# PSUM tiles by row pair, an earlier way out, and whole-array products for the first chunk in a convolution-and-feed-forward kernel

## The chip, the cores and the metric

The kernel runs on one core of a Trainium2 chip. The metric is the device time of one execution in microseconds (us); of several timed executions the median is given.

## The reference, cut to what matters

The input `x` has 4 sequences of 4096 tokens with 192 numbers each. A softmax over 7 taps, one set for each token and each of 8 heads, weighs the token and the six before it; a two-layer network with 2048 hidden units follows.

```python
w = softmax(weight_gen, axis=-1)                  # (4, 4096, 8, 7)
out[b, s, h, :] = sum over k of w[b, s, h, k] * x_pad[b, s + k, h, :]   # 6 zero rows ahead
h = out.reshape(16384, 192) @ w_in                # 192 -> 2048
g = maximum(0.01 * h, h)
y = g @ w_out                                     # 2048 -> 192
```

## The kernel before, in words

**Tiling.** Each of the 128 partitions owns 128 consecutive tokens. A chunk is 4 of these rows for all partitions, 512 tokens; there are 32 chunks (`NCH`). The inner size is cut into 16 blocks of 128 (`NF`), taken two at a time, which gives 8 steps for a chunk (`NQ`) and 256 in all (`NP`). Step q is step i = q mod 8 of chunk c = q div 8; its two blocks are numbers 2q and 2q+1.

**Precision.** Each fp32 value goes to TensorE as the sum of two parts, `h` and `l`. The first product (`mm1`) needs h·h, h·l and l·h for three blocks of 64 of the 192 inputs. The second (`mm2_pass`) multiplies the high part of the activations (`g_h`) by both parts of `w_out` (384 columns) and the low part (`g_l`) by the high one (192 columns).

**TensorE (PE).** All products but the first transposes use the array as two halves of 64 rows, which work at the same time on different PSUM banks. The second product of one block is made in four passes. In pass i the upper half works on one of the four rows of tokens and the lower half on another; passes 0 and 1 give each row one half of its sum, passes 2 and 3 the other. I call the two matmul pairs of one block in one pass (384 columns, then 192) a *set*; a block has 4 sets, a chunk 64. Passes 0 and 1 (`mm2_first`) end a step, passes 2 and 3 (`mm2_second`) follow the first product of the next step. Between them `tell` places a nop on SyncE (SP) that waits for the last matmul of pass 1; pass 2 waits for this nop. SP also issues nearly all DMAs, in order.

**A chunk's boundary.** `firsts` says which blocks a step begins. Step i = 1 begins none, it finishes the old chunk's last two blocks and then calls `evacuate`; step i = 2 begins four blocks of the new chunk. The sums of four rows lie in one PSUM tile of four banks (`po`, one buffer). `evacuate` takes rows 0 and 2 as one strided slice and rows 1 and 3 as another: ScalarE (ACT) copies the low columns to `ot`, VectorE (DVE) adds the high ones, one DMA stores four rows.

**Activations.** `act(n)` is a Prelu in place in PSUM and a copy to `g_h` on ACT, then a subtraction to `g_l` on DVE. PSUM holds four tiles `hp` of the first product; `g_h` and `g_l` have six buffers each.

**The next chunk's input.** The convolution runs on GpSimd (POOL). Its result is split (`split_h` on ACT, `split_l` on POOL), transposed in blocks of 32 on DVE (`squares`), and spread over the partitions by 16 DMAs from SP into `xx` (`spread_squares`, four for each k). From chunk 2 on a chunk's convolution result is split at i = 1, squared at i = 2 and spread at i = 3 to 6 of the chunk before it.

**The start.** The weights arrive as 64-bit numbers and are rounded and split by ACT, DVE and POOL while chunk 0 is computed. The order of all this work is written out by hand in `START`: a letter is one piece of work, `s` is the next step. `x` and `X` spread chunks 1 and 2, `m` and `Y` are their last squares, `v` and `V` their `split_l`, `w` widens a weight block and issues a later block's load on SP, `o` and `O` round, `q` is one operation of a convolution on POOL. The tile framework makes an instruction wait for earlier ones that touch the same part of a tile, or, for a new tile, the same buffer.

Of the kernel before, what the change touches and what calls it, by code (L numbers as in the profile page):

```python
# [24 lines left out]

C0 = 1

START = "ASgdeddeedddggedregpwpdgdrwegggekeodgggeedoegrgedupedlprruwTrowlpulwsKwroupOswlpuLopsrUlOwrppsuOrwlupowrrOulwwlrOuplpoMscuwutlrwvosumrEowlorLulwuODquqqqqLqqxssqLqqqqqssssCyVqqqqsqqqqqqqYqqXsss"


@with_exitstack
def conv_attention_moe_kernel(
# [291 lines left out]
                    start=(m == 0), stop=(m == len(passes) - 1),  # L324
                )

    def act(n):

        t = hp.pop(n)
        nc.scalar.activation(out=t, in_=t, func=AF.Prelu, alpha=0.01)  # L330
        g_h[n] = gp.tile([P, TOK], F32R, tag="gh", name="gh")
        g_l[n] = gp.tile([P, TOK], F32R, tag="gl", name="gl")
        h, l = g_h[n], g_l[n]
        if n >= NF:
            t = t.rearrange("p (k j t) -> p j k t", k=NK, j=J)
            h, l = (g.rearrange("p (j k t) -> p j k t", k=NK, j=J) for g in (h, l))
        nc.scalar.copy(out=h, in_=t)  # L337
        nc.vector.tensor_tensor(out=l, in0=t, in1=h.bitcast(F32), op=ALU.subtract)  # L338

    po = {}  # L340
    count = dict(mm2=0)
    after = mybir.DependencyInfo(mybir.DependencyClass.Sync, mybir.DependencyReason.DATA)
    HALF = J // 2

    def mm2_pass(ns, i, told=None):

        rows = range(J)[::1 if count["mm2"] % 2 else -1]
        for n in ns:  # L350
            f = n % NF
            for g, d in ((g_h, 2 * D), (g_l, D)):
                for u, s in enumerate(HALVES):
                    j = rows[(i + u * HALF) % J]
                    ins = nc.tensor.matmul(  # L355
                        out=po[0][:, j, 0:d],
                        lhsT=g[n][s, j * P:(j + 1) * P], rhs=wo[s, f, 0:d],
                        start=(f == 0 and i < HALF and g is g_h),
                        stop=(f == NF - 1 and i >= HALF and g is g_l),
                        skip_group_check=True,  # L360
                    ).ins
                    if told is not None:
                        tc.add_manual_dep(ins, told.name, after, reason="rows left")
                        told = None
        return ins
# [7 lines left out]
    def mm2_first(ns):  # L373


        if ns[0] % NF == 0:
            po[0] = ps_o.tile([P, J, TOK], F32, tag="o", name="po")
        count["mm2"] += 1
        for i in range(HALF):
            ins = mm2_pass(ns, i)  # L380
        return tell(ins)

    def mm2_second(ns, told):
        for i in range(HALF, J):
            mm2_pass(ns, i, told if i == HALF else None)
        for n in ns:
            del g_h[n], g_l[n]

    def last_products(ns):

        count["mm2"] += 1
        told = [None] * HALF
        for i in range(J):
            ins = mm2_pass(ns, i, told[i - HALF] if i >= HALF else None)
            if i < HALF:
                told[i] = tell(ins)

    def evacuate(c, last=False):


        ot = op.tile([P, J, D], F32, tag="ot", name="ot")
        r = row_of(c)
        even, odd = slice(0, J, 2), slice(1, J, 2)
        for i, js in enumerate((even, odd) if count["mm2"] % 2 else (odd, even)):
            nc.scalar.copy(out=ot[:, js], in_=po[0][:, js, D:2 * D])  # L405
            nc.vector.tensor_tensor(  # L406
                out=ot[:, js], in0=po[0][:, js, 0:D], in1=ot[:, js], op=ALU.add
            )
            if last:
                eng = (nc.sync, nc.scalar)[i]  # L410
                eng.dma_start(out=out_rows[:, r + js.start:r + J:2, :], in_=ot[:, js])
        if not last:
            nc.sync.dma_start(out=out_rows[:, r:r + J, :], in_=ot)

    order = [(0, IN), (1, IN), (2, IN), (0, OUT)]
    for q in range(3, NQ):
# [18 lines left out]
    with tc.manual_schedule():  # L435
# [31 lines left out]

        def firsts(q):

            c, i = divmod(q, NQ)  # L470
            if i == 1 or q == 0:
                return []
            if i == 0:
                return list(range(2 * q - (4 if c == 1 else 2), 2 * q))
            if c == 0:
                return [2 * q - 4, 2 * q - 3]
            if q == NP - 1:
                return []
            return list(range(2 * q - (4 if i == 2 else 2), 2 * q))

        def step(q):

            c, i = divmod(q, NQ)
            if i == 0 and c in sm_q:
                load_weights(sm_q[c])
                load_rows(sm_q[c])
            if i == 1 and c in sm_q:
                softmax_max(sm_q[c])
                softmax_sub(sm_q[c], nc.gpsimd)
            begun, told = pending.pop() if pending else (None, None)  # L490
            mm1(q)


            if c != 1 or i != 1:
                act(2 * q)
# [4 lines left out]
            if c == 1 and i == 1:  # L500
                act(2 * q)
            act(2 * q + 1)
            ns = firsts(q)
            if ns:
                pending.append((ns, mm2_first(ns)))
            if c > 1:
                if i == 0:
                    feed(c + 1, 2 * K)
                if c + 1 < NCH:
                    if i == 1:  # L510
                        split_h(c + 1)
                        split_l(c + 1, nc.gpsimd)
                    if i == 2:
                        squares(c + 1, 0)
                        squares(c + 1, 1)
                    if 3 <= i < 3 + NK:
                        spread_squares(c + 1, [i - 3])
# [8 lines left out]
        w0 = ps_o.tile([P, J, TOK], F32, tag="o", name="w0")  # L526
# [7 lines left out]
        n = 0  # L534
        for what in START:
            if what in stages:
                prepare(what)
# [26 lines left out]
            elif what in "cC":  # L564
                split_h(1 + "cC".index(what))
            elif what in "vV":
                split_l(1 + "vV".index(what), nc.gpsimd)
            elif what in "tm":
                squares(1, "tm".index(what))
            elif what in "yY":  # L570
                squares(2, "yY".index(what))
            elif what in "xX":
                spread_squares(1 + "xX".index(what))
            elif what == "s":
                step(n)
                n += 1
# [37 lines left out]
```

## Time and profile before

| | |
|---|---|
| median of 3 runs | 1223.44 us (1222.64 to 1223.48) |
| profiled execution | 1225.84 us, its span 1224.1 us |
| mean granted TensorE clock | 0.988 |
| PE busy | 1159.2 us, 95% of the span |
| POOL / ACT / DVE busy | 798.5 (65%) / 655.7 (54%) / 518.5 (42%) us |
| chain that ended last | PE 83%, DVE 5%, ACT 5%, SP's queue 3%, DMA 2%, issue 2% |

Busy time is a share over the whole span; of a matmul the start is recorded and the end modelled, so that the distance from start to start tells what a matmul takes out of the stream. The chain that ended last is followed back from the last instruction to what released it, step by step.

### The profile page before, as it was taken

The page shows a single profiled execution, that of the slowest core. Times are in us where ns is not written, and L with a number is a line of the kernel's source. Part 1 is how long each engine was busy: PE and PEld are TensorE (multiplying, and loading weights), DVE is VectorE, ACT ScalarE, POOL GpSimd, SP SyncE. Part 2 cuts the span into 40 slices and gives each one's busy share as a digit, 9 for nine tenths or more (in the row PEclk, how much of TensorE's full clock was granted, in tenths as well). Part 3 has the DMA queues.
Part 4 walks back from the last instruction along what each step waited for, and adds up shares of the span by engine and source line. Part 5 has one row for each costly group of instructions (what it writes and reads, how often), then busy time and mean ns, then how long its engine had stood idle before and what let it go on. Part 6 is the DMA issues. An engine that isn't in the chain of part 4 may idle for free.

```text
span 1224.1 us, 30487 instructions
## 1 busy us (share of the span) xinstructions
PE 1159.2 (95%) x12812; PEld 1047.6 (86%) x12812; DVE 518.5 (42%) x857; ACT 655.7 (54%) x1187; POOL 798.5 (65%) x511
## 2 busy tenths in 40 slices
PE   2778999999999999999999999999999999999997
PEld 1667988999889898898898988888889989898887
DVE  7753343344444343444343444434344433443432
ACT  3645455455555555555555555545555554555553
POOL 7778666776666678666677766658766667965300
PEclk9799999999999999999999999999999999999999
DMA  6342032322313242232323313232231323222120
GB/s 195 104 118 66 28 106 65 106 66 52 106 50 108 53 118 67 53 96 52 116 53 84 92 48 106 53 105 66 67 99 49 103 66 105 66 54 52 47 59 14
DMA packets 39366, 95.29 MB, mean 78 GB/s; under 512 B 9407, under 2 KB 17087, under 8 KB 37438
## 3 DMA queue, kind: packets, MB, share of 16 engines
q1 hardware_dynamic: 38542, 92.77, 27.4%
q8 instruction: 100, 1.64, 0.6%
q10 hardware_dynamic: 688, 0.59, 0.2%
q14 instruction: 36, 0.29, 0.1%
HBM read 31.98 MB, written 12.58 MB: 36 GB/s over the span
## 4 chain that ended last, share of the span: by engine, by line
PE 83%; DVE 5%; ACT 5%; SPq 3%; issue 2%; DMA 2%; DVEq 0%; ACTq 0%
PE po L355 45%; PE hp L322 38%; DVE ot L406 3%; SPq L305 2%; ACT ot L405 2%; ACT gh L337 1%; ACT hp L330 1%; DMA xx<-sq 1%; DVE gl L338 0%; DMA wi_raw<-in_moe_w_in_dram 0%; DVE t L118 0%; DVE t L116 0%; DVE bits L122 0%; DVE acc L250 0%; DMA wt<-in_weight_gen_dram 0%
## 5 line engine op out<-in xcount | busy, mean ns | idle before, releaser
L355 PE MATMUL po<-wo,gh 64*128 64x384 f32 x4096 | 615.7, 356 | 21.9 <-SPq L369 11.1
L338 DVE TENSOR_TENSOR gl<-hp,gh 128x512 fp32r<-128x512 f32 x512 | 354.0, 691 | 666.8 <-ACT gh L337 666.4
L330 ACT ACTIVATE hp<-hp 128x512 f32<-128x512 f32 x512 | 301.3, 589 | 458.2 <-PE hp L322 458.2
L355 PE MATMUL po<-wo,gl 64*128 64x192 f32 x4096 | 535.2, 250 | 0.8 <-DVE gl L338 0.6
L322 PE MATMUL hp<-xx,wi_h 64*128 64x512 f32 x3072 | 514.5, 400 | 14.7 <-DVE bits L122 4.5
L355 PEld LDWEIGHTS po<-wo,gh 64*128 64x128 f32 x4096 | 411.6, 185 | 45.6 <-PE hp L322 23.6
L355 PEld LDWEIGHTS po<-wo,gl 64*128 64x128 f32 x4096 | 414.1, 188 | 13.0 <-DVE gl L338 1.8
L250 POOL TENSOR_TENSOR acc<-acc,tmp 128x768 f32<-128x768 f32 (+1 forms) x191 | 346.9, 1816 | 14.3
L322 PEld LDWEIGHTS hp<-xx,wi_h 64*128 64x128 f32 x3072 | 300.9, 186 | 60.9 <-DVE gl L338 6.0
L322 PE MATMUL hp<-xx,wi_l 64*128 64x512 f32 x1536 | 334.0, 394 | 0.0
L337 ACT CAST gh<-hp 128x512 fp32r<-128x512 f32 x512 | 300.7, 587 | 48.0 <-PE po L355 33.0
L240 POOL TENSOR_TENSOR tmp<-xt,wt 128x768 f32<-128x768 f32 (+1 forms) x192 | 290.4, 1513 | 12.1
L322 PEld LDWEIGHTS hp<-xx,wi_l 64*128 64x128 f32 x1536 | 171.1, 186 | 29.3
L286 POOL TENSOR_TENSOR split<-acc,split 128x768 fp32r<-128x768 f32 x31 | 57.1, 1842 | 200.1 <-ACT split L282 200.1
L203 POOL TENSOR_TENSOR wt<-wt,mx 128x448 f32<-128x448 f32 x15 | 14.6, 973 | 72.7 <-DVE mx L200 72.6
L295 DVE STREAM_TRANSPOSE sq<-split 128x384 f32<-128x384 f32 x124 | 60.6, 545 | 0.0
L405 ACT COPY ot<-po 128x384 f32<-128x384 f32 x64 | 30.7, 480 | 34.6 <-DVE ot L406 23.4
L240 POOL TENSOR_TENSOR acc<-xt,wt 128x768 f32<-128x768 f32 (+1 forms) x32 | 48.4, 1514 | 0.2
L406 DVE TENSOR_TENSOR ot<-po,ot 128x384 f32<-128x384 f32 x64 | 35.4, 554 | 26.4 <-ACT ot L405 26.4
L216 POOL TENSOR_TENSOR wt<-wt,sm 128x448 f32<-128x448 f32 (+1 forms) x16 | 15.5, 971 | 38.4 <-DVE sm L213 38.4
L282 ACT CAST split<-acc 128x768 fp32r<-128x768 f32 x31 | 26.0, 838 | 0.7 <-POOL acc L250 0.7
L269 PE MATMUL ta<-ident,twice 128*128 128x128 f32 x12 | 2.8, 423 | 21.6 <-DVE twice L245 21.6
(43 smaller groups left out, 148.9 us busy)
## 6 DMA issues: line engine op xcount, KB each, us to landing
xx<-sq SPq DMA_DIRECT2D x496, 96.0 KB, 2.2
xt<-in_x_dram SPq DMA_DIRECT2D x14, 1344.0 KB, 5.8
out_dram<-ot SPq DMA_DIRECT2D x31, 384.0 KB, 2.3
wt<-in_weight_gen_dram SPq DMA_DIRECT2D x16, 224.0 KB, 2.6
wo_raw<-in_moe_w_out_dram SPq DMA_DIRECT2D x8, 384.0 KB, 3.5
wi_raw<-in_moe_w_in_dram SPq DMA_DIRECT2D x14, 192.0 KB, 3.5
xt<-in_x_dram SPq DMA_DIRECT2D x1, 960.0 KB, 5.3
xt<-in_x_dram SPq DMA_DIRECT2D x1, 768.0 KB, 6.1
```

The costliest lines, as they stand in the source:

```text
L240: eng.tensor_tensor(out=ov, in0=xv, in1=wk, op=ALU.mult)
L250: eng.tensor_tensor(out=acc, in0=acc, in1=out, op=ALU.add)
L282: nc.scalar.copy(out=split[c][:, 0], in_=att[c])
L286: eng.tensor_tensor(out=l, in0=att.pop(c), in1=h.bitcast(F32), op=ALU.subtract)
L295: nc.vector.transpose(out=sq[c][:, v, i], in_=src[:, v])
L322: nc.tensor.matmul(out=hp[2 * q + u], lhsT=w[s], rhs=r[s], start=(m == 0), stop=(m == len(passes) - 1),)
L330: nc.scalar.activation(out=t, in_=t, func=AF.Prelu, alpha=0.01)
L337: nc.scalar.copy(out=h, in_=t)
L338: nc.vector.tensor_tensor(out=l, in0=t, in1=h.bitcast(F32), op=ALU.subtract)
L355: ins = nc.tensor.matmul(out=po[0][:, j, 0:d], lhsT=g[n][s, j * P:(j + 1) * P], rhs=wo[s, f, 0:d], start=(f == 0 and i < HALF and g is g_h ...
L405: nc.scalar.copy(out=ot[:, js], in_=po[0][:, js, D:2 * D])
L406: nc.vector.tensor_tensor(out=ot[:, js], in0=po[0][:, js, 0:D], in1=ot[:, js], op=ALU.add)
```

## The change

Rows 0 and 1 get one PSUM tile of two banks, rows 2 and 3 another, and the passes pair the rows accordingly. Prelu and split are separate functions; at a boundary the order on ACT is now Prelu of the first block, copies of `evacuate`, then the rest. `mm2_first` goes block by block, no longer pass by pass. In chunk 0 the second product uses all 128 rows of the array (`mm2_whole`): one matmul in place of a pair, no second half, no nop; it is evacuated at step 8, no longer at step 9. The spreading of chunks from 3 on begins at i = 2; in `START`, `X` is two groups of eight DMAs, one before step 13 and one before step 14, and `Y` and one `O` stand earlier.

```diff
-START = "...uOrwlup...ODquqqqqLqqxssqLqqqqqssssCyVqqqqsqqqqqqqYqqXsss"
+START = "...OrppsurwlupODquqqqqLqqxxxxssqLqqqqqssssCyVqqqqqqYqqqsqXXqqsXXsssq"
...
-    def act(n):
+    def leak(n):
+        return nc.scalar.activation(out=hp[n], in_=hp[n], func=AF.Prelu, alpha=0.01).ins
+    def split_g(n):
         t = hp.pop(n)
-        nc.scalar.activation(out=t, in_=t, func=AF.Prelu, alpha=0.01)
...
+    def new_sums():
+        for i in range(2):
+            po[i] = ps_o.tile([P, J // 2, TOK], F32, tag=f"o{i}", name="po")
+    ROWS_OF = (0, 2, 1, 3)
...
-        rows = range(J)[::1 if count["mm2"] % 2 else -1]
+        rows = ROWS_OF[::1 if count["mm2"] % 2 else -1]
...
-                        out=po[0][:, j, 0:d],
+                        out=po[j // HALF][:, j % HALF, 0:d],
...
     def mm2_first(ns):
...
-        for i in range(HALF):
-            ins = mm2_pass(ns, i)
-        return tell(ins)
+        for n in ns:
+            for i in range(HALF):
+                ins = mm2_pass([n], i)
+        return ins
...
+    def mm2_whole(ns):
+        if ns[0] == 0:
+            new_sums()
+        for n in ns:
+            for j in range(J):
+                for g, d in ((g_h, 2 * D), (g_l, D)):
+                    nc.tensor.matmul(
+                        out=po[j // HALF][:, j % HALF, 0:d],
+                        lhsT=g[n][:, j * P:(j + 1) * P], rhs=wo[:, n, 0:d],
+                        start=(n == 0 and g is g_h), stop=(n == NF - 1 and g is g_l),
+                        skip_group_check=True,
+                    )
+            del g_h[n], g_l[n]
     def last_products(ns):
         count["mm2"] += 1
-        told = [None] * HALF
-        for i in range(J):
-            ins = mm2_pass(ns, i, told[i - HALF] if i >= HALF else None)
-            if i < HALF:
-                told[i] = tell(ins)
+        for i in range(HALF):
+            mm2_pass(ns[:2], i)
+        told = [tell(mm2_pass(ns[2:], i)) for i in range(HALF)]
+        for i in range(HALF, J):
+            mm2_pass(ns, i, told[i - HALF])
     def evacuate(c, last=False):
...
+        for i in range(2):
+            k = i if count["mm2"] % 2 else 1 - i
+            ot = op.tile([P, HALF, D], F32, tag="ot", name="ot", bufs=2)
+            nc.scalar.copy(out=ot, in_=po[k][:, :, D:2 * D])
+            nc.vector.tensor_tensor(out=ot, in0=po[k][:, :, 0:D], in1=ot, op=ALU.add)
+            eng = nc.scalar if last and i == 1 else nc.sync
+            eng.dma_start(out=out_rows[:, r + k * HALF:r + (k + 1) * HALF, :], in_=ot)
...
             mm1(q)
+            leak(2 * q)
             if begun:
                 mm2_second(begun, told)
                 if begun[-1] % NF == NF - 1:
                     evacuate(begun[-1] // NF)
+            split_g(2 * q)
+            leak(2 * q + 1)
+            split_g(2 * q + 1)
+            if c == 0 and i >= 2:
+                mm2_whole([2 * q - 4, 2 * q - 3])
+            elif q == NQ:
+                mm2_whole(range(2 * q - 4, 2 * q))
+                evacuate(0)
+            elif c > 0 and firsts(q):
+                ns = firsts(q)
+                pending.append((ns, tell(mm2_first(ns))))
...
-                    if 3 <= i < 3 + NK:
-                        spread_squares(c + 1, [i - 3])
+                    if 2 <= i < 2 + NK:
+                        spread_squares(c + 1, [i - 2])
...
             elif what in "xX":
-                spread_squares(1 + "xX".index(what))
+                u = "xX".index(what)
+                spread_squares(1 + u, [spreads[u]])
+                spreads[u] += 1
```

## Rows read from the trace of the kernel before

**Rows 1.** The view of waits over the whole span, three of PE's waits: who waited for whom, us in total, times, longest.
```profile
PE po L355 <- SPq L369: 11.1, 3, 5.0
PE po L355 <- DVE ot L406: 10.8, 31, 0.4
...
PE hp L322 <- DMA xx<-sq: 4.1, 5, 1.3
```

**Rows 2.** Busy time of PE in two stretches that together are one chunk's period: from the first product of step i = 3 (chunk 16) to that of i = 1 of the next chunk, and from there to its i = 3; the third row is a stretch of the start. Columns: stretch, its length, PE busy us (instructions), granted clock, DMA share, GB/s.
```profile
611.03:638.50 27.47, 27.47 (x321) 1.00 0.25 59
638.50:646.93 8.43, 8.01 (x88) 1.00 0.13 49
...
80.90:83.90 3.00, 3.00 (x24) 0.50 0.02 5
```

**Rows 3.** The chain that ended last, one boundary of chunks in order of time: start, us, what.
```profile
606.22 0.49 ACT ot L405
...
606.74 0.57 DVE ot L406
...
607.33 0.49 ACT ot L405
...
607.84 0.57 DVE ot L406
...
611.20 2.12 PE hp L322 x18
```

**Rows 4.** The timeline of PE, ACT and DVE at the same boundary: start, us, engine, line, operation, tiles, and in brackets the idle time before it and its releaser.
```profile
607.91 0.39 PE L322 MATMUL hp<-xx,wi_l 64*128 64x512 f32 x1
608.55 0.44 PE L355 MATMUL po<-wo,gh 64*128 64x384 f32 x2 [0.24 <-DVE ot L406]
...
604.88 0.58 ACT L330 ACTIVATE hp<-hp 128x512 f32<-128x512 f32 x1 [2.07 <-PE hp L322]
...
608.95 0.69 DVE L338 TENSOR_TENSOR gl<-hp,gh 128x512 fp32r<-128x512 f32 x1 [0.55 <-ACT gh L337]
```

**Rows 5.** The timeline of PE: the first matmuls of steps 16 and 248 (i = 0 of chunks 2 and 31).
```profile
129.79 0.66 PE L322 MATMUL hp<-xx,wi_h 64*128 64x512 f32 x4
1177.54 0.65 PE L322 MATMUL hp<-xx,wi_h 64*128 64x512 f32 x4
```

**Rows 6.** The timeline of SP's queue in the start: weight loads, then the 16 DMAs of `x`, then the 16 of `X`; a row's time spans its xN issues.
```profile
53.10 12.13 SPq L95 DMA_DIRECT2D wo_raw<-in_moe_w_out_dram  x3
69.38 10.13 SPq L305 DMA_DIRECT2D xx<-sq  x16
111.04 10.06 SPq L305 DMA_DIRECT2D xx<-sq  x16
```

**Rows 7.** The timeline of PE in the start: the three waits for the nop, each with what follows; the first matmuls of steps 8, 11, 14 and 15.
```profile
65.34 0.44 PE L355 MATMUL po<-wo,gh 64*128 64x384 f32 x2 [2.52 <-SPq L369]
79.62 0.45 PE L355 MATMUL po<-wo,gh 64*128 64x384 f32 x2 [3.56 <-SPq L369]
80.88 0.58 PE L355 MATMUL po<-wo,gh 64*128 64x384 f32 x2
83.02 1.11 PE L322 MATMUL hp<-xx,wi_h 64*128 64x512 f32 x4
99.60 0.66 PE L322 MATMUL hp<-xx,wi_h 64*128 64x512 f32 x4
113.92 0.65 PE L322 MATMUL hp<-xx,wi_h 64*128 64x512 f32 x4
121.21 0.69 PE L355 MATMUL po<-wo,gh 64*128 64x384 f32 x2 [5.01 <-SPq L369]
125.41 0.65 PE L322 MATMUL hp<-xx,wi_h 64*128 64x512 f32 x4
```

**Rows 8.** The timelines of ACT and DVE in the start: a copy to `g_h` that waits for PE, and the last squares of chunk 1.
```profile
66.45 0.59 ACT L337 CAST gh<-hp 128x512 fp32r<-128x512 f32 x1 [3.00 <-PE po L355]
...
68.78 1.03 DVE L295 STREAM_TRANSPOSE sq<-split 128x384 f32<-128x384 f32 x2
```

**Rows 9.** Weight loads (PEld) and matmuls of PE: the only whole-array work of the trace (the first transposes), and a few rows of second products in halves.
```profile
21.55 2.79 PE L269 MATMUL ta<-ident,twice 128*128 128x128 f32 x12 [21.55 <-DVE twice L245]
...
613.33 0.26 PE L355 MATMUL po<-wo,gl 64*128 64x192 f32 x2
613.61 0.26 PE L355 MATMUL po<-wo,gl 64*128 64x192 f32 x2
...
613.33 0.20 PEld L355 LDWEIGHTS po<-wo,gh 64*128 64x128 f32 x2
```

**Rows 10.** Squares and spreading in a later chunk: DVE's timeline, SP's timeline, and the durations of one issue of line 305 (min/median/max in ns, first and last start).
```profile
612.50 1.95 DVE L295 STREAM_TRANSPOSE sq<-split 128x384 f32<-128x384 f32 x4
616.91 15.49 SPq L305 DMA_DIRECT2D xx<-sq  x16
L305 SPq DMA_DIRECT2D xx<-sq x496: 507/590/1938, 69.4 to 1175.2; - x166
```

**Rows 11.** The chain that ended last, its end: start, us, what.
```profile
1214.46 3.82 PE po L355 x50
...
1218.30 0.49 ACT ot L405
...
1218.81 0.57 DVE ot L406
```

More of the change, by code (lines that the diff above doesn't have):

```diff
@@ L26 @@
 C0 = 1
-START = "ASgdeddeedddggedregpwpdgdrwegggekeodgggeedoegrgedupedlprruwTrowlpulwsKwroupOswlpuLopsrUlOwrppsuOrwlupowrrOulwwlrOuplpoMscuwutlrwvosumrEowlorLulwuODquqqqqLqqxssqLqqqqqssssCyVqqqqsqqqqqqqYqqXsss"
+START = "ASdegddeedddggedregpwpdgdrwgeggekedgggeoedoegrgedupedlprruwTrowlpulwsKwroupOswlpuLopsrUlOwOrppsurwlupowrrOulwwlrOuplpoMscuwutlrwvosumrEwlorLulwouODquqqqqLqqxxxxssqLqqqqqssssCyVqqqqqqYqqqsqXXqqsXXsssq"
 @with_exitstack
@@ L338, in act @@
         nc.vector.tensor_tensor(out=l, in0=t, in1=h.bitcast(F32), op=ALU.subtract)
-    po = {}
+    po = [None, None]
+    def new_sums():
+        for i in range(2):
+            po[i] = ps_o.tile([P, J // 2, TOK], F32, tag=f"o{i}", name="po")
     count = dict(mm2=0)
@@ L376, in mm2_first @@
         if ns[0] % NF == 0:
-            po[0] = ps_o.tile([P, J, TOK], F32, tag="o", name="po")
+            new_sums()
         count["mm2"] += 1
-        for i in range(HALF):
-            ins = mm2_pass(ns, i)
-        return tell(ins)
+        for n in ns:
+            for i in range(HALF):
+                ins = mm2_pass([n], i)
+        return ins
     def mm2_second(ns, told):
@@ L387, in mm2_second @@
             del g_h[n], g_l[n]
+    def mm2_whole(ns):
+        if ns[0] == 0:
+            new_sums()
+        for n in ns:
[8 more added lines that the diff above has]
+            del g_h[n], g_l[n]
     def last_products(ns):
         count["mm2"] += 1
-        told = [None] * HALF
-        for i in range(J):
-            ins = mm2_pass(ns, i, told[i - HALF] if i >= HALF else None)
-            if i < HALF:
-                told[i] = tell(ins)
+        for i in range(HALF):
[3 more added lines that the diff above has]
+            mm2_pass(ns, i, told[i - HALF])
     def evacuate(c, last=False):
-        ot = op.tile([P, J, D], F32, tag="ot", name="ot")
         r = row_of(c)
[L403 to L413, printed above, removed]
+        for i in range(2):
[5 more added lines that the diff above has]
+            eng.dma_start(out=out_rows[:, r + k * HALF:r + (k + 1) * HALF, :], in_=ot)
     order = [(0, IN), (1, IN), (2, IN), (0, OUT)]
@@ L468, in firsts @@
         def firsts(q):
[L470 to L479, printed above, removed]
+            i = q % NQ
+            return range(2 * q - (4 if i == 2 else 2), 2 * q if i != 1 and q < NP - 1 else 0)
         def step(q):
@@ L499, in step @@
                     evacuate(begun[-1] // NF)
[L500 to L505, printed above, removed]
+            split_g(2 * q)
[9 more added lines that the diff above has]
+                pending.append((ns, tell(mm2_first(ns))))
             if c > 1:
@@ L524, in step @@
                 softmax_div(sm_q[c], nc.gpsimd)
-        w0 = ps_o.tile([P, J, TOK], F32, tag="o", name="w0")
+        w0 = ps_o.tile([P, J // 2, TOK], F32, tag="o0", name="w0")
         w0 = w0[:, 0, 0:J * HK].rearrange("p (h k) -> p h k", k=K)
@@ L533, in conv_attention_moe_kernel @@
         )
-        n = 0
+        n, spreads = 0, [0, 0]
         for what in START:
```

2 lines of the change are left out of this document (removed).

## The prediction

> **What bounds the kernel now.** I read the page first: PE is busy 95% of the span, the next engine 65%. So the time is PE's stream plus PE's gaps, and the waits of PE are read next [rows 1]: three waits for the nop on SP (11.1 us), 31 for `ot` on DVE, one at each boundary of chunks (10.8 us), five for the spread input (4.1 us). What a gap costs I take from the distance between starts.
>
> The steady part: one period is 27.47 + 8.43 = 35.90 us [rows 2]. The first stretch has six first products and 52 sets (12 at step 3, then five times 8) and no gap. A first product takes 2.12 us [rows 3], so a set takes (27.47 − 6 × 2.12) / 52 = 0.284 us. The second stretch has two first products and 12 sets, which makes 4.24 + 3.41 = 7.65 us, but takes 8.43: 0.78 us are lost at each boundary, more than the 0.35 us (10.8 / 31) that the waits show. From the last pair of the first product (607.91, the next would start 0.23 later) to the first set (608.55) there are 0.4 us; the rest is a second hold, where the last block's `g_l`, which DVE begins only at 608.95, is needed, and the two halves of the array falling into step again [rows 4]. The chain names the cause: copy, addition, copy, addition, strictly one after the other from 606.22 to 608.41 [rows 3]. The second copy waits for the first addition because both write interleaved rows of one `ot`, and the first waits for the last pass for the same reason in `po`.
>
> Steps 16 to 248 are 29 periods and take (1177.54 − 129.79) / 29 = 36.13 us each [rows 5], 0.23 more than 35.90: 6.6 us in all, in the chunks in which the wait for the spread input falls; issues that take up to 1.94 us in place of 0.59 [rows 10] make the last four DMAs late.
>
> **The change part by part.** *Boundary.* With a tile for each row pair, copy A can start when pass 2 ends, one pass of two blocks (0.57 us) before pass 3. The Prelu occupies ACT from 604.88 to 605.46 [rows 4]; copy A then runs 605.5 to 606.0, its addition to 606.6, copy B from 606.2, where the first copy stood [rows 3], to 606.7, its addition to 607.3. PE wants the tiles at about 608.0. The wait goes, with 0.6 us to spare. The ACT work moved behind the copies: cast of the first block to 607.3, Prelu and cast of the second to 608.4, `g_l` by 609.1, earlier than now. Block by block, the fourth block of step 2 starts three times 0.57 us after 608.0, at 609.7, so `g_l` is in time. Bounds: 0.35 us (only what the view of waits shows) to 0.78; I take 0.78, because both holds end in the same chain. 30 boundaries (chunk 0's is counted below) × 0.78 = 23.4 us, at least 10.5. The second output DMA is one issue more on SP in a stretch in which SP waits anyway: nothing.
>
> *Spreading from i = 2.* The last four DMAs go one step (2.12 + 8 × 0.284 = 4.39 us) earlier, the waits are at most 1.3 us [rows 1]: all 6.6 us go, at least the 4.1. The price: at i = 2 SP now waits for the squares (to 614.45), then issues four DMAs (2.4 us, to 616.9), and the nop of step 3 is queued behind; PE needs it when the first product of step 4 is through, at 618.7 [rows 10] (step 3 begins at 611.03 and takes 2.12 + 12 × 0.284 + 2.12 to that point). Slack 1.8 us now, some 1.3 when PE's boundary is 0.78 us shorter and DVE's work 0.3: nothing.
>
> *The start.* Before, the nop of step 5 is queued behind three weight loads (12.13 us on SP), that of step 7 behind the 16 DMAs of `x` [rows 6, 7]. Whole-array products have no nop. A copy to `g_h` that waited 3.0 us for PE [rows 8] no longer does; the weight preparation around it runs on ACT, POOL and DVE in order and hardly moves, so the last squares of chunk 1, at 68.78 to 69.8, go to about 66.2 to 67.2. 16 issues take 10.1 us [rows 6] and a landing 2.2 (the page's part 6): step 8 can start at 79.5 in place of 83.02 [rows 7]. PE has by then done steps 6 and 7 and idled about 3.5 us. A gap of 3.56 us was followed, from 80.88 on, by a granted clock of 0.50, the lower level of 1.2 GHz, for over 3 us [rows 2, 7]; so the first product of step 8 may take 3.4 us. Then 16 whole sets 4.55, two first products 4.24, eight sets 2.27: step 11 at 94.0 where 99.60 stands [rows 7]; 5.6 us gained, the double copying at chunk 0's boundary included.
>
> The nop of step 13 was behind all 16 DMAs of `X`: step 14 took 125.41 − 113.92 = 11.5 us in place of 4.4 (5.0 idle, the rest at the lower clock) [rows 7]. Now eight DMAs (5.05 us) stand before the nop of step 13 and eight before that of step 14. In the new time: nop of step 12 at 103.6, DMAs to 108.7, nop 13 (needed at 110.0), DMAs to 113.9, nop 14 (needed at 114.4). It fits with 0.5 us to spare: 7.1 us gained. The earlier `Y` waits for `split_l` on POOL about as long as DVE is free. Together 12.7 us; bounds 6 (only `X`, with a small wait left) and 16.
>
> *Whole array.* Its only cost on the path is at step 8: 16 sets, taken at 0.284 us like the pairs. A whole-array pair streams the same 384 and 192 columns. In halves a load starts together with a matmul of the same tile and the next set follows 0.28 us later [rows 9], so the load runs beside the stream. The nearest whole-array row is the transposes, 2.79 / 12 = 0.23 us for load and 128 columns, at the start of the kernel, unlike in type; two such as a set's extra would be at most 0.46. Bounds 0.25 to 0.75 us for a set; I take 0.284, from the row nearest in operands. A change between halves and whole array is not in the trace; a matmul's modelled duration exceeds the distance to the next by some 0.16 us (0.39 against 0.235 in first products), and 2 × 0.16 at step 8 is within the bounds.
>
> The Trainium skill (TensorEngine Tiling (Array Packing), Key Properties) says that changing the tiling mode drains TensorE. No run here shows it; with the 0.16 us above as the price of a drain, 14 changes would be 2.2 us, of which only those of step 8 have no cover.
>
> *The end.* `last_products` does passes 0 and 1 of two blocks before it needs the last `g_l` at 1214.46: two sets, 0.57 us. Copy A and its addition (0.49 + 0.57) run beside pass 3, so of 2.2 us after the products 1.1 remain [rows 11]. 1.6 us; bounds 0.6 and 1.8.
>
> *Sum.* 23.4 + 6.6 + 12.7 + 1.6 = 44.3 us off the span of 1224.1, which leaves 1179.8. The profiled execution took 1225.84, 1.8 above its span; the median of the runs, 1223.44, is 2.4 below that execution. I take the gain off the median: 1179.1 us. The lower bounds together (10.5 + 4.1 + 6 + 0.6 = 21.2) give 1202, the upper ones (23.4 + 6.6 + 16 + 1.8 = 47.8) 1176.
>
> **The rivals.** *Half the boundary.* The evacuation is out of the way, but the second hold stays, because ACT now has both copies ahead of the cast and `g_l` of the last block comes after PE wants it. For it: ACT's chain at the boundary is seven pieces of 0.5 to 0.6 us in line. Against: my times leave 0.6 us. Only 10.5 to 12 us of 23.4 then: about 1191.
>
> *The whole array waits for its loads.* If a load can't run beside a matmul in the same rows, a set takes 0.284 + 2 × 0.20 (a load's duration, [rows 9]) = 0.68 us: 16 × 0.4 = 6.4 us at step 8, and of 3.2 us at each of six steps about 4 us uncovered: 1189. Against it speaks that in halves load and matmul overlap.
> The Trainium skill (TensorE: Matmul & The Clock Gate, Part 3) says that weight loads overlap with matmuls in flight only when the row group differs, which is this case. By that rule the time is this rival's; in halves the trace does not agree, since both halves load and multiply at the same time.
>
> *SP holds the nop of step 3* (the slower side). The squares must be done before four DMAs, and the nop stands behind these. If the squares or issues (up to 1.94 us each) came later than my times by more than 1.3 us, PE would wait for the excess in each of 30 chunks. It outweighs the other gains from 1.3 + 44.3 / 30 = 2.8 us on; at 3.0 us later the time is 1223 + 6 = 1229. For it: DVE's squares stand in line behind two `g_l`. Against: only the slowest issues reach this, in four chunks of 29.
>
> *It doesn't do what it says*: the framework still holds both tiles until both additions are done, and PE waits as before at the boundary; the other parts remain: 1203.
>
> **How the numbers follow.** Forecast 62% (its own range 1173 to 1187, from the start's bounds and a set's), half the boundary 17%, loads 9%, no effect at the boundary 6%, SP's hold 4%, the rest (a wait in the start that I don't see) 2%. A range from 1172 to 1196 leaves out the two cases above it and the tail below. Faster by over 0.2% (2.4 us, about what a measurement can tell): all but SP's hold and a part of the rest, 95%; within 0.2%: 2%; slower: 3%.
>
> **What would show it.** A period of 35.1 us between steps of the same kind; no wait of PE for `ot`; the second copy without a wait for the first addition. No wait of PE for the nop before step 8; step 11 near 94 and step 16 near 117. No wait for `xx` after chunk 1. Whole sets 0.28 us apart. I am wrong if the period stays above 35.5, if step 16 starts after 122, or if PE waits for SP at steps 4, 14 or 15.

## The result, and the profile after

The changed kernel takes **1180.5 us** (median of 4 runs, 1179.7 to 1182.49), the kernel before beside it 1223.04 us (1222.42 to 1223.48): a ratio of 0.9655, 95% interval 0.9638 to 0.9672. The forecast was 1179.1 us.

The busy times of the page of the changed kernel (its span is 1177.9 us) and its chain by engine; PE's busy share is 97% now, and ACT, 5% of the chain before, is 1%:

```profile
PE 1139.8 (97%) x12684; PEld 1026.5 (87%) x12684; DVE 522.1 (44%) x857; ACT 653.7 (55%) x1187; POOL 797.6 (68%) x511
...
PE 93%; DVE 3%; SPq 2%; ACT 1%; DMA 1%; issue 0%; DVEq 0%; ACTq 0%
```

The view of waits, two of PE's (us, times, longest). They answer to [rows 1]: the 31 waits for `ot` are gone, of three waits for the nop one is left, of five for the spread input one, and that one is chunk 1's:

```profile
PE hp L322 <- DMA xx<-sq: 0.8, 1, 0.8
PE po L365 <- SPq L379: 0.7, 1, 0.7
```

PE in the two stretches of one chunk, cut at the same places as [rows 2]: from step i = 1 to i = 3, and from there to the next i = 1. The first stretch took 8.43 us and now takes 7.62 without a gap; the other has not changed:

```profile
612.08:619.70 7.62, 7.62 (x88) 1.00 0.15 54
619.70:647.17 27.47, 27.47 (x321) 1.00 0.37 98
```

The timeline of PE, ACT and DVE at that boundary, to be laid beside [rows 4]:

```profile
614.39 0.58 ACT L328 ACTIVATE hp<-hp 128x512 f32<-128x512 f32 x1 [2.08 <-PE hp L322]
...
614.95 1.05 ACT L431 COPY ot<-po 128x384 f32<-128x384 f32 x2
...
615.46 1.13 DVE L432 TENSOR_TENSOR ot<-po,ot 128x384 f32<-128x384 f32 x2 [2.42 <-ACT ot L431]
...
615.89 0.60 ACT L339 CAST gh<-hp 128x512 fp32r<-128x512 f32 x1
...
617.43 0.34 PE L365 MATMUL po<-wo,gh 64*128 64x384 f32 x2
...
617.63 0.69 DVE L340 TENSOR_TENSOR gl<-hp,gh 128x512 fp32r<-128x512 f32 x1 [0.42 <-ACT gh L339]
```

The two copies are one row now (x2, 1.05 us): the second starts when the first ends and waits for no addition. The additions end at 616.59; PE wants the tiles at 617.43, 0.23 us after the start of its last pair of first products (617.20), so 0.84 us are to spare. The last `g_l` is there at 618.32, the fourth block begins three times 0.57 us after 617.43.

The first matmuls of steps 8, 11, 14, 15 and 16, and the one wait for a nop, with [rows 7] as their counterpart. Of step 8 one matmul runs at 75.96; all others stand behind the wait for chunk 1's input, so I take 77.19 for step 8 of this kernel from here on:

```profile
75.96 0.46 PE L322 MATMUL hp<-xx,wi_h 64*128 64x512 f32 x1 [1.53 <-DVE gl L340]
77.19 0.69 PE L322 MATMUL hp<-xx,wi_h 64*128 64x512 f32 x3 [0.77 <-DMA xx<-sq]
...
92.29 0.65 PE L322 MATMUL hp<-xx,wi_h 64*128 64x512 f32 x4
...
106.60 0.65 PE L322 MATMUL hp<-xx,wi_h 64*128 64x512 f32 x4
...
110.98 0.65 PE L322 MATMUL hp<-xx,wi_h 64*128 64x512 f32 x4
...
114.01 0.44 PE L365 MATMUL po<-wo,gh 64*128 64x384 f32 x2 [0.74 <-SPq L379]
...
116.38 0.65 PE L322 MATMUL hp<-xx,wi_h 64*128 64x512 f32 x4
```

**Where the 46.2 us of span (1224.1 to 1177.9) come from.** Step 16 starts at 116.38, not at 129.79: 13.4 us. From there to the last step the period is 35.09 us in every chunk, not 35.90 with some chunks longer: 30 boundaries × 0.81 = 24.3 us, and the 6.6 us that the chunks with a wait for `xx` cost. From the start of the last step to the end of the span it is 1.9 us shorter (15.00 to 13.07). 13.4 + 24.3 + 6.6 + 1.9 = 46.2. These are two single executions: the one profiled before took 2.8 us more than its median, the one after 0.8 less than its own, and the medians are 42.5 us apart. If the later terms are the same in every run, the start is worth some 9.7 us by the medians (an estimate: 42.5 less 32.8). The runs that follow take the large terms one by one.

### The profile page after: what moved, and what is told of

The parts are those of the page before. It is cut to its first block, busy times and chain, and to the rows that moved or that the text cites. A ratio compares the mean times of both kernels' runs of the same rounds, so it can differ in the third digit from the quotient of the medians.

```text
span 1177.9 us, 30385 instructions
## 1 busy us (share of the span) xinstructions
PE 1139.8 (97%) x12684; PEld 1026.5 (87%) x12684; DVE 522.1 (44%) x857; ACT 653.7 (55%) x1187; POOL 797.6 (68%) x511
## 4 chain that ended last, share of the span: by engine, by line
PE 93%; DVE 3%; SPq 2%; ACT 1%; DMA 1%; issue 0%; DVEq 0%; ACTq 0%
PE po L365 47%; PE hp L322 45%; SPq L305 2%; DVE gl L340 1%; DVE t L118 0%; PE po L407 0%; ACT hp L328 0%; DMA wi_raw<-in_moe_w_in_dram 0%; DVE t L116 0%; DVE bits L122 0%; DVE bits L130 0%; ACT gh L339 0%; DVE acc L250 0%; DMA wt<-in_weight_gen_dram 0%; DVE h L240 0%
## 5 line engine op out<-in xcount | busy, mean ns | idle before, releaser
L365 PE MATMUL po<-wo,gh 64*128 64x384 f32 x3968 | 581.3, 353 | 0.7 <-SPq L379 0.7
L322 PE MATMUL hp<-xx,wi_h 64*128 64x512 f32 x3072 | 497.6, 398 | 11.0 <-DVE gl L340 4.7
L365 PE MATMUL po<-wo,gl 64*128 64x192 f32 x3968 | 497.5, 247 | 0.3 <-DVE gl L340 0.3
L365 PEld LDWEIGHTS po<-wo,gl 64*128 64x128 f32 x3968 | 378.1, 187 | 11.2 <-DVE gl L340 0.5
L365 PEld LDWEIGHTS po<-wo,gh 64*128 64x128 f32 x3968 | 372.2, 184 | 13.0 <-SPq L379 1.2
L322 PEld LDWEIGHTS hp<-xx,wi_h 64*128 64x128 f32 x3072 | 275.4, 186 | 63.4 <-DVE gl L340 7.0
L322 PE MATMUL hp<-xx,wi_l 64*128 64x512 f32 x1536 | 311.9, 394 | 0.0
L322 PEld LDWEIGHTS hp<-xx,wi_l 64*128 64x128 f32 x1536 | 150.6, 186 | 34.4
```

What stands on the lines that cost most here:

```text
L322: nc.tensor.matmul(out=hp[2 * q + u], lhsT=w[s], rhs=r[s], start=(m == 0), stop=(m == len(passes) - 1),)
L365: ins = nc.tensor.matmul(out=po[j // HALF][:, j % HALF, 0:d], lhsT=g[n][s, j * P:(j + 1) * P], rhs=wo[s, f, 0:d], start=(f == 0 and i < HA ...
```

## The experiments

### The boundary alone, and its opposite in one step each

`d_boundary` is the kernel before with the boundary's part only: the two tiles and `ROWS_OF`, block by block, the order on ACT. `START`, the spreading, chunk 0's products in halves and the order of the last products stay as before.

```diff
-            po[0] = ps_o.tile([P, J, TOK], F32, tag="o", name="po")
+            new_sums()
...
-                act(2 * q)
+            leak(2 * q)
             if begun:
...
+            split_g(2 * q)
```

> The kernel before with the boundary's part alone (two PSUM tiles, row pairs, ACT order, block by block; the start, the spreading and the end as before). Theory: the whole 0.78 to 0.81 us at each of 30 boundaries goes, so 1223 - 24 = 1199 us; period 35.1 us; the waits for xx stay, 4 to 7 us in all, in the same chunks. Rival (the start made the difference and the boundary is worth only the 0.35 us of the view of waits): 1212 us, period 35.5.

Measured: 1198.77 us (1196.87 to 1200.81) beside 1224.34; ratio 0.9797, 0.9779 to 0.9814. The period is 35.09 us in its shortest chunks. 1224.34 × 0.0203 = 24.8 us, where the prediction says 23.4 for 30 boundaries. Two more evacuations gain by the new tiles: chunk 0's (steps 8 to 11 take 14.75 us here, 16.58 before, 15.44 in `d_order` below) and the last one (13.78 us from the start of the last step to the end, 15.00 before). The other waits have stayed, as the view of waits shows:

```profile
PE po L365 <- SPq L379: 11.1, 3, 5.0
...
PE hp L322 <- DMA xx<-sq: 3.6, 7, 0.9
```

So the boundary is worth more than half of the whole gain, and it doesn't need the other parts. Which of its edits does it? Five kernels ask this, each timed once beside one run of the kernel before; their periods are read from the profiles.

`d_order` is the kernel before with the new order on ACT alone: Prelu, copies, then the casts.

```diff
-            if c != 1 or i != 1:
-                act(2 * q)
+            leak(2 * q)
             if begun:
...
-            act(2 * q + 1)
+            split_g(2 * q)
+            leak(2 * q + 1)
+            split_g(2 * q + 1)
```

> The kernel before with the ACT order of the change alone (Prelu, copies, then casts; one PSUM tile, interleaved rows). Theory: the first copy waits for the end of pass 3 and the second for the first addition whatever stands behind them, so nothing is gained: 1223 us, period 35.9. Rival (leaving ahead of the activations is what helps): period 35.5 or less, 1211 or less.

Measured: 1232.84 us beside 1225.45, with a period of 36.22 us in its shortest chunks: slower, which neither theory had. The view of waits and two rows of PE at a boundary:

```profile
PE po L357 <- DVE gl L340: 9.1, 32, 0.3
```

```profile
645.43 0.44 PE L357 MATMUL po<-wo,gh 64*128 64x384 f32 x2 [0.24 <-DVE ot L408]
...
647.07 0.35 PE L357 MATMUL po<-wo,gl 64*128 64x192 f32 x2 [0.28 <-DVE gl L340]
```

The copies still wait for one another, and now the casts stand behind them. PE still waits for `ot`, and 1.6 us later a second time, for `g_l`. This is the rival "half the boundary" in the flesh: it exists, but only while the copies are held up.

`u_rows` is the changed kernel with one PSUM tile, the old pairing of rows and one `ot`; the order on ACT and block by block stay.

```diff
-        for i in range(2):
-            po[i] = ps_o.tile([P, J // 2, TOK], F32, tag=f"o{i}", name="po")
+        po[0] = ps_o.tile([P, J, TOK], F32, tag="o", name="po")
...
-    ROWS_OF = (0, 2, 1, 3)
+    ROWS_OF = (0, 1, 2, 3)
...
+        ot = op.tile([P, J, D], F32, tag="ot", name="ot")
...
+        even, odd = slice(0, J, 2), slice(1, J, 2)
```

> The changed kernel with one PSUM tile and the old pairing of rows 0 with 2 and 1 with 3, interleaved slices of one ot. Theory: the serial chain of copy, addition, copy, addition is back, and with it most of the loss: period 35.6 to 35.9, 1195 to 1204 us. Rival (order and block by block do the work): period 35.1, 1180.

Measured: 1197.47 us beside 1225.45, period 35.60 us, 30 waits of PE for `ot` (7.1 us). As expected. It also shows that block by block is worth (36.22 − 35.60) = 0.62 us in a chunk when the boundary is tight, since `d_order` differs from it there by this, and by where the spreading begins, which moves the shortest period by 0.02 us (35.07 in `u_spread`). With the first passes pass by pass, the last block's `g_l` is wanted three sets, 0.85 us, earlier.

`u_tile` keeps the new pairing and two `ot`, and takes back only the split of the PSUM tile: rows 0 and 1 are one contiguous slice of the tile of four banks, rows 2 and 3 the other.

```diff
-        for i in range(2):
-            po[i] = ps_o.tile([P, J // 2, TOK], F32, tag=f"o{i}", name="po")
+        po[0] = ps_o.tile([P, J, TOK], F32, tag="o", name="po")
...
-                        out=po[j // HALF][:, j % HALF, 0:d],
+                        out=po[0][:, j, 0:d],
...
+            rs = slice(k * HALF, (k + 1) * HALF)
-            nc.scalar.copy(out=ot, in_=po[k][:, :, D:2 * D])
+            nc.scalar.copy(out=ot, in_=po[0][:, rs, D:2 * D])
```

> The changed kernel with one PSUM tile of four banks, but the new pairs of rows (contiguous slices) and two ot tiles. Theory: waits go by the rows that an instruction touches, so the first copy still leaves after pass 2 and nothing changes: period 35.1, 1180 us. Rival (waits go by tile): the first copy waits for pass 3 and starts 0.7 us later; the last addition then ends about when PE wants the tile, period 35.1 to 35.3, 1180 to 1187.

Measured: 1197.2 us, period 35.60 us, as much as `u_rows`. The timeline of ACT and PE at one boundary:

```profile
623.61 0.48 ACT L431 COPY ot<-po 128x384 f32<-128x384 f32 x1 [0.57 <-PE po L364]
...
624.71 0.48 ACT L431 COPY ot<-po 128x384 f32<-128x384 f32 x1 [0.62 <-DVE ot L432]
...
625.93 0.45 PE L364 MATMUL po<-wo,gh 64*128 64x384 f32 x2 [0.24 <-DVE ot L432]
```

The first copy reads rows that pass 3 doesn't write, and still waits 0.57 us, until pass 3 is through. The second copy waits 0.62 us for the first addition, though it reads other banks and writes another `ot`. So the interleaved rows were not the cause, against the prediction: what is kept in order is the accesses to one PSUM *tile*, whichever rows they touch, and even two that only read it, as this addition and this copy do. The rows lie in four banks with one tile as with two, so it is the waits that go with a tile, not the banks, that differ. The text ahead says that an instruction waits for earlier ones that touch the same *part* of a tile; for these PSUM tiles that is wrong. Pairing, contiguous rows and two `ot` buy nothing while there is one tile; splitting it buys 35.60 − 35.09 = 0.51 us in a chunk. Whether a single `ot` beside two PSUM tiles would bring the hold back was not tried.

`u_order` is the changed kernel with the first block's cast ahead of the copies again, `u_pass` the one with the first passes pass by pass.

```diff
             leak(2 * q)
+            split_g(2 * q)
             if begun:
...
-            split_g(2 * q)
```

> The changed kernel with the cast of the first block again ahead of the copies at a boundary. Theory: the copies start 0.6 us later, the last addition ends about when PE wants the tiles (607.9 to 608.0 in the time of the rows before), so at most 0.15 us is lost at a boundary: period 35.1 to 35.25. Rival (the order is what makes the room): period 35.4 or more, over 1189 us.

```diff
-        for n in ns:
-            for i in range(HALF):
-                ins = mm2_pass([n], i)
+        for i in range(HALF):
+            ins = mm2_pass(ns, i)
```

> The changed kernel with mm2_first again pass by pass. Theory: the fourth block of step 2 is wanted 0.85 us after the first products' end, its g_l is ready about 0.25 us later than that: period 35.2 to 35.4, 1183 to 1190 us. Rival (g_l is early enough once the copies are out of the way): period 35.1.

Measured, both beside 1226.49 us: 1182.63 us with a period of 35.10 for the order, 1181.91 us with 35.11 to 35.13 for the passes. That is 0.01 and 0.02 to 0.04 us in a chunk, for `u_pass` less than expected. Once the tiles are split, the 0.84 us to spare swallow both. So the parts don't add up one by one: from 36.22 (`d_order`) block by block takes 0.62 and the split 0.51; from 35.09 backwards block by block is worth 0.03.

### The spreading

`u_spread` is the changed kernel with the spreading back at i = 3 to 6.

```diff
-                    if 2 <= i < 2 + NK:
-                        spread_squares(c + 1, [i - 2])
+                    if 3 <= i < 3 + NK:
+                        spread_squares(c + 1, [i - 3])
```

> The changed kernel with the spreading again at i = 3 to 6. Theory: the last four DMAs are late in the same chunks as before, 6.6 us come back: 1187 us, with waits of PE for xx of 0.5 to 1.6 us in four places. Rival (the waits were a consequence of the boundary's stalls): 1180.5 and no such wait.

Measured: 1188.64 us (1187.51 to 1190.04), ratio 0.9714, 0.97 to 0.9729; some 8 us over the changed kernel. Steps 17 to 249 (29 periods) take 1024.93 us, in the changed kernel 1017.70: 7.2 us more, where 6.6 were forecast. The view of waits has the cause:

```profile
PE hp L322 <- DMA xx<-sq: 3.5, 6, 0.9
```

One of the six waits is chunk 1's, as in the changed kernel; the five others show 2.5 us of the 7.2. The rest doesn't show as waits: 13 of the 29 chunks are longer, by 0.2 to 1.1 us, each at its step i = 0 and two at the step before as well. They are not the chunks of before, as the theory had it: there it is six, and four of these are among the 13.

The landings say why so little is enough. In the trace of the kernel before, the last of a chunk's 16 DMAs lands 0.02 to 0.18 us ahead of that chunk's step i = 0 in 23 of 29 chunks, and 0.4 to 1.5 us after it in the six others. In the changed kernel it lands 3.1 to 4.6 us ahead in all of them.

### `X` in two groups

`u_X` is the changed kernel with all 16 DMAs of `X` before step 13.

```diff
-START = "...YqqqsqXXqqsXXsssq"
+START = "...YqqqsqXXXXqqssssq"
```

> The changed kernel with all 16 DMAs of X ahead of the nop of step 13. Theory: the nop goes out some 10 us after the first of them, about 4.5 us after PE wants it, and PE then runs for over 3 us at the lower clock: step 14 takes 10 to 11 us, and the time is 1186 us. Rival (SP has room, since Y stands earlier): 1180.5.

Measured: 1186.37 us (1184.35 to 1187.7), ratio 0.9691, 0.967 to 0.971: some 6 us over the changed kernel. SP's queue and PE in the timelines:

```profile
105.12 10.38 SPq L305 DMA_DIRECT2D xx<-sq  x16
```

```profile
109.14 0.65 PE L322 MATMUL hp<-xx,wi_h 64*128 64x512 f32 x4
...
115.62 0.69 PE L365 MATMUL po<-wo,gh 64*128 64x384 f32 x2 [4.19 <-SPq L379]
...
119.42 0.65 PE L322 MATMUL hp<-xx,wi_h 64*128 64x512 f32 x4
```

The nop stands behind 10.4 us of issues, PE waits 4.19 us for it, and the step takes 10.28 us. In the changed kernel step 14 takes 4.38 us and step 15, which has the short wait, 5.40. The mechanism of [rows 7] is the one that was removed.

### The whole array in chunk 0

`u_whole` is the changed kernel with chunk 0's second products in halves and with nops, and `firsts` as before; the new `START` stays. `u_whole5` and `after5` are the same kernel and the changed kernel, timed again in five rounds on one chip.

```diff
-            if c == 0 and i >= 2:
-                mm2_whole([2 * q - 4, 2 * q - 3])
-            elif q == NQ:
-                mm2_whole(range(2 * q - 4, 2 * q))
-                evacuate(0)
-            elif c > 0 and firsts(q):
+            if firsts(q):
```

> The changed kernel with chunk 0's second products in halves again, with nops, evacuated at step 9. Theory: the nops of steps 5 and 7 are again behind weight loads and the 16 DMAs of x, the copies to g_h wait again, and step 11 starts 4 to 6 us later, near 97: 1185 us. Rival (the gain of the start is the order in START and the move of X alone): step 11 near 92, 1180.5.

> The changed kernel itself, timed on the chip of the next run: 1180.5 us, within 2 us.

> The changed kernel with chunk 0 in halves, beside the changed kernel on one chip. Theory now: the whole array saves what step 11 showed in the profiles, less what the granted clock of the first steps (which differs from run to run) brought in; 1.5 to 3.5 us slower than the changed kernel, not the 5 first expected. Rival (it is worth nothing, and the difference of 1.6 between medians on two chips was noise): within 1 us.

Measured: 1182.1 us (1181.02 to 1184.38), ratio 0.9663, 0.9646 to 0.9679; in five rounds 1181.82 (1179.75 to 1183.81; ratio 0.9655, 0.9641 to 0.9669) against 1180.19 for the changed kernel (1179.8 to 1182.51; ratio 0.9648, 0.9635 to 0.9662). The intervals overlap, so the times alone don't show that the whole array is worth anything; by the medians it would be 1.6 us, and in the profiles step 16 comes 1.7 and 3.2 us later without it. I had expected 1185 and step 11 near 97; it was at 94.15 (95.90 in `u_whole5`). The nops do come late, as PE's timeline in `u_whole` shows:

```profile
62.44 0.69 PE L365 MATMUL po<-wo,gh 64*128 64x384 f32 x2 [2.49 <-SPq L379]
...
77.47 0.44 PE L365 MATMUL po<-wo,gh 64*128 64x384 f32 x2 [2.80 <-SPq L379]
```

Why do 5.3 us of waits buy so little? DVE's last squares of chunk 1 tell: in the changed kernel they start at 63.98, in `u_whole` at 66.62. PE's nop waits did hold them up, through the copy to `g_h`, as forecast; ACT's timeline in `u_whole` shows that copy:

```profile
64.29 0.59 ACT L339 CAST gh<-hp 128x512 fp32r<-128x512 f32 x1 [3.95 <-PE po L365]
```

From chunk 1's first squares to its last ones it takes 7.46 us in both profiles with halves and the new `START`, and 3.88 to 4.65 us in all nine with the whole array: the effect is real, and 2.8 us or more in this place. But what ends the wait of step 8 in the changed kernel is the landing of the DMAs behind these squares:

```profile
63.98 1.03 DVE L295 STREAM_TRANSPOSE sq<-split 128x384 f32<-128x384 f32 x2
```

```profile
64.57 10.79 SPq L305 DMA_DIRECT2D xx<-sq  x16
```

Squares, 10.8 us of issues, 2.2 us of flight (74.78 to 76.96 in the chain), step 8 at 77.19. In `u_whole` step 8 hangs on the same queue: the last sets before it wait until 77.47 for the nop behind the 16 issues, which end at 77.35. So PE gains at step 8 what the squares gain, 79.84 − 77.19 = 2.65 us, and not the sum of its waits. And it gives back 0.8 us at once: steps 8 to 11 take 14.31 us in halves and 15.10 with the whole array (from 77.19), whose step 8 comes after waits of PE (1.53 and 0.77 us) and begins at a granted clock of 0.64, a mean of stretches at either level, 1.2 and 2.4 GHz:

```profile
77.00:80.60 3.60, 3.41 (x18) 0.64 1.01 385
```

Step 11 doesn't settle the size either. In six profiles whose work is the same up to there (the two of the changed kernel, `u_spread`, `u_X`, `u_order`, `u_pass`) it starts at 92.29 to 94.83, a spread as wide as what is to be measured; `u_whole` has 94.15 and `u_whole5` 95.90.

### The whole array everywhere

`w_all` uses `mm2_whole` in every chunk, with no nop left. It is a probe of what the whole array costs, not a proposal.

```diff
-            elif q == NQ:
-                mm2_whole(range(2 * q - 4, 2 * q))
-                evacuate(0)
-            elif c > 0 and firsts(q):
-                ns = firsts(q)
-                pending.append((ns, tell(mm2_first(ns))))
+            elif c > 0 and i != 1 and q < NP - 1:
+                mm2_whole(range(2 * q - (4 if q == NQ or i == 2 else 2), 2 * q))
+                if i == 0:
+                    evacuate(c - 1)
```

> The changed kernel with whole-array second products in all chunks (no halves and no nops there). Theory: a whole set takes 0.288 us as a pair does, and each pass from halves to whole array and back costs some 0.45 us (0.31 before the first whole matmul, 0.08 in it, 0.09 behind the last); seven a chunk: period 38.2 us, 1275 us. Rival 1 (loads can't run beside matmuls of the same rows): a set of 0.68, period 60. Rival 2 (the change of mode hides once the queue is full): period 35.1, 1180.

Measured: 1257.6 us beside 1225.45, period 37.67 us. A chunk has seven changes into whole-array products and seven back, so one there and back costs (37.67 − 35.09) / 7 = 0.37 us. PE's timeline around one of them, in `w_all`, and around a change of products in halves, in the changed kernel:

```profile
503.78 0.40 PE L322 MATMUL hp<-xx,wi_l 64*128 64x512 f32 x2
504.11 0.44 PE L408 MATMUL po<-wo,gh 128*128 128x384 f32 x1
504.39 0.25 PE L408 MATMUL po<-wo,gl 128*128 128x192 f32 x1
504.47 0.36 PE L408 MATMUL po<-wo,gh 128*128 128x384 f32 x1
...
508.49 0.36 PE L408 MATMUL po<-wo,gh 128*128 128x384 f32 x1
508.69 0.25 PE L408 MATMUL po<-wo,gl 128*128 128x192 f32 x1
508.87 0.72 PE L322 MATMUL hp<-xx,wi_h 64*128 64x512 f32 x4
509.43 0.39 PE L322 MATMUL hp<-xx,wi_l 64*128 64x512 f32 x2
```

```profile
613.96 0.39 PE L322 MATMUL hp<-xx,wi_l 64*128 64x512 f32 x2
614.19 0.34 PE L365 MATMUL po<-wo,gh 64*128 64x384 f32 x2
614.37 0.25 PE L365 MATMUL po<-wo,gl 64*128 64x192 f32 x2
...
615.23 0.25 PE L365 MATMUL po<-wo,gl 64*128 64x192 f32 x2
615.32 0.65 PE L322 MATMUL hp<-xx,wi_h 64*128 64x512 f32 x4
615.80 0.39 PE L322 MATMUL hp<-xx,wi_l 64*128 64x512 f32 x2
```

Read the distances between starts: 0.33 against 0.23 into the second product, 0.28 against 0.18 for its first matmul, 0.18 against 0.09 on the way back, 0.56 against 0.48 for the first matmuls after it. The differences (0.10, 0.10, 0.09, 0.08) are the 0.37. In between, 14 whole sets from 504.47 to 508.49 are 0.287 us apart, as are six in halves in the changed kernel (617.70 to 619.42).

The Trainium skill (TensorEngine Tiling (Array Packing), Key Properties) says that a change of the tiling mode drains TensorE; this trace agrees, with 0.37 us there and back, a little over the 0.32 that the prediction took for two changes.

## Why the prediction was right, and where it was not

**Boundary, 23.4 us: the size was right (24.3), the cause was not.** The step that failed is "the second copy waits for the first addition because both write interleaved rows of one `ot`, and the first waits for the last pass for the same reason in `po`". `u_tile` has neither interleaved rows nor a shared `ot` and has both waits (0.57 and 0.62 us). The tile is the unit, and had the change only re-paired the rows, some 15 of the 24 us (30 × 0.51) would not have come. The choice of 0.78 us instead of the 0.35 that the waits show was right: the whole 0.81 went. Copy A started at the Prelu's end, as reckoned; the margin was 0.84 us, not 0.6, and the two copies came back to back.

**Spreading, 6.6 us:** 7.2 by `u_spread`, and PE waits for no nop at step 3 of any chunk; the price was nothing, as forecast. The reason given, slow issues, holds for four of the six late chunks before. In the other two (chunks 21 and 28) the last issue ended in time and the landing came 3.2 and 2.9 us after it, in place of 1.6; and issues of 1.8 to 1.9 us made no chunk late elsewhere (11, 20, 23, 30). The waits themselves went, as forecast.

**The start, 12.7 us: 13.4 in the two profiles, some 9.7 by the medians.** Step 8 came at 77.19, not 79.5, and step 11 at 92.29, not 94.0, so 7.3 us were gained up to there where 5.6 were forecast. The chain behind the 5.6 (nop, copy, squares, DMAs, step 8) is real: from chunk 1's first squares to its last ones 6.73 us became 3.88, a gain of 2.9 for a forecast of 2.6. The term that was off is the time of the last squares, 63.98 in place of 66.2, and that is not the change alone. Already the first squares come 1.95 us earlier (62.05 to 60.10), and such a difference needs no change of the kernel: up to step 8 `d_order` has the same instructions as the kernel before, in the same order on ACT, DVE, POOL and SP, and yet its first squares start at 58.05 and its step 8 at 79.95, 3.1 us before that of the kernel before. The two part in step 0, which no edit touches: pairs of 512 columns are 0.43 us apart there in the kernel before and 0.23 in `d_order`. PE's timelines of the one and the other:

```profile
27.64 1.48 PE L322 MATMUL hp<-xx,wi_h 64*128 64x512 f32 x4
```

```profile
26.57 0.86 PE L322 MATMUL hp<-xx,wi_h 64*128 64x512 f32 x4
```

From the first squares on the profiles can be compared: to step 11 it is 37.55 us before, 37.34 in `d_order`, 36.70 in `d_boundary`, 36.56 and 34.99 with halves and the new `START`, and 31.86 to 34.16 in the six with the whole array (32.19 in the changed kernel). So 5.4 of the 7.3 us fall here. The six with the whole array take 33.1 us on the mean, the two with halves 35.8; chunk 0's boundary takes 0.7 to 1.8 us off steps 8 to 11. That the prediction laid the gain mainly to products without a nop is borne out in this stretch; the times of the runs do not show it. In step 0 all nine profiles with the whole array run at the pace of the kernel before, and both of `u_whole` at that of `d_order`; whether that is chance or goes with the program stays open. `START` also moves two `g` and two `o` by a few letters, which the text ahead doesn't name; neither these nor the earlier `Y` and `O` were tried alone.

**`X`, 7.1 us:** the step "it fits with 0.5 us to spare" failed by 1.2 us: PE waits 0.74 us at step 15, one of the three waits named as signs of an error. SP began its 16 issues at 102.58, 1.0 earlier than reckoned, and ended them at 113.90 as reckoned, mostly because one took 1.53 us in place of 0.59. PE, 1.1 us ahead of the forecast by then, was there first. The chain of waits shows it:

```profile
111.09 1.53 SPq L305
...
113.31 0.59 SPq L305
...
114.01 2.54 PE po L365 x32
```

Steps 11 to 15 gained 7.1 us (25.81 to 18.69), and 1.0 was lost again in the next step (5.40 in place of 4.39). `u_X` puts the edit's worth at some 6 us of the whole time.

**Whole sets at 0.284 us:** 0.287. The mode change, costed at 0.16 us each, came to 0.37 for two.

**The end, 1.6 us:** 1.9, of which 0.58 are the products (3.82 to 3.24 us after the last `g_l`) and 1.1 the copy and addition that now run beside them. Pass 3's products end at 1173.4 and one copy and one addition follow, as [rows 11] without its first pair.

**The sum.** The time came out 1.4 us above the forecast, which is luck in part: the gain between the medians was 42.5 us for 44.3, with 0.9 more at the boundaries, 0.3 more at the end and, by the estimate above, some 3 less in the start. The forecast had read its terms from an execution 2.4 us above the median.

**The rivals.** Half the boundary: its mechanism showed in `d_order` only. The whole array waiting for its loads: its signature, sets 0.68 apart, is nowhere; in the changed kernel a load of whole-array weights starts together with a matmul over the same 128 rows:

```profile
82.10 0.25 PE L407 MATMUL po<-wo,gl 128*128 128x192 f32 x1
82.10 0.19 PEld L407 LDWEIGHTS po<-wo,gh 128*128 128x128 f32 x1
82.19 0.36 PE L407 MATMUL po<-wo,gh 128*128 128x384 f32 x1
```

The Trainium skill (TensorE: Matmul & The Clock Gate, Part 3) says that such loads overlap only when the row group differs. These rows differ from that: both work on all 128 rows, and the matmul of the new weights starts 0.09 us after. (The prediction's "which is this case" is to be read as: the products of this case all use the same rows, so their loads would have to wait.)

SP holding the nop of step 3 and the change doing nothing at the boundary both fell: the view of waits has none of PE's between 140 and 1170 us.

## What to carry to other kernels

When two engines empty one PSUM tile in pieces, give each piece a tile of its own: here the accesses to a tile were kept in order as a whole, and slices, row orders and output buffers changed nothing until the tile was split. A wait that the profile shows as 0.35 us cost 0.81; price a gap by the distance between starts around it, and price an edit with its neighbours in place, since the order on ACT was a loss alone (36.22 us) and free beside the split. An instruction that others wait for should not stand behind a batch of DMAs on the same queue, and slack in that queue should cover one issue of 1.5 us.

## What the runs showed of the hardware that I had not expected

- The first steps run at a different pace from profile to profile, with the same work. In step 0, from the first matmul to the first Prelu, it is 4.0 to 4.6 us in ten of the fourteen profiles and 2.8 to 3.0 in four (`d_order`, `d_boundary`, `u_whole`, `u_whole5`), though the granted clock of 24 to 31 us reads 1.00 in all. From 36 to 48 us its mean over both levels was 0.70 in the kernel before, 0.86 in the changed kernel (both profiles), 1.00 in `d_boundary` and `u_spread`, and 0.89 to 0.90 in `u_whole` and `u_whole5`. Step 16 of one and the same kernel fell at 116.38 and 116.47, of another (`u_whole`) at 118.05 and 119.69.
- Going from halves to the whole array and back costs 0.37 us, spread over four distances of about 0.1 us each, while a set within the whole array costs the same as in halves (0.287 us).
